# The second pair's last tile of a bilinear MLP as seven block products: its gate and up taken as the two rows of blocks, its weights summed anew, and the last output row written in halves

## The chip, the cores and the metric

The kernel runs on one core of a Trainium2 chip. The metric is the device time of one execution in microseconds. Three runs of the kernel before took 871.22, 871.30 and 872.47 us; the median is 871.3. A further execution was taken with the hardware profiler on and took 871.17 us; all rows below come from it. TensorE does the matmuls (PE; PEld is its weight load), VectorE (DVE), ScalarE (ACT) and GpSimd (POOL) do elementwise work, SyncE (SP) issues nearly all DMAs.

## The reference

All in float32, for one sequence of 2048 rows of 512. A layer norm with a shift and scale from a conditioning vector, a segmented attention with a memory (four segments of 512 rows), its residual, and then a second layer norm and a bilinear MLP with 1376 hidden columns:

```python
def _B_ref(x, w_gate, w_up, w_down):
    g = jnp.einsum("bsd,df->bsf", x, w_gate)
    u = jnp.einsum("bsd,df->bsf", x, w_up)
    h = g * u
    return jnp.einsum("bsf,fd->bsd", h, w_down)
...
    h = _layernorm(x, axis=-1) * (1 + ca) + sa
    x = x + ga * _A_ref(h, A_wq, A_wk, A_wv, A_wo, A_beta)
    h = _layernorm(x, axis=-1) * (1 + cb) + sb
    x = x + gb * _B_ref(h, B_w_gate, B_w_up, B_w_down)
```

Only the MLP is touched by the change.

## The kernel before, in words

**Precision.** A float32 product is made of three fast ones: each operand is split into a high part (`wh`, `bh`, a ScalarE copy that rounds) and a low part (`wl`, `bl`, a VectorE subtraction), and high by high, low by high and high by low are added up. Two halves of the contraction make it six matmuls (`six`, line 1259), always into one PSUM bank of 512 columns.

**Tiles.** The 2048 rows are four segments of 512, taken as two pairs, p = 0 and 1, with c = 0 and 1 for the segment in the pair. The 1376 hidden columns are tiles of 128, numbers 0 to 10; tile 10 (`LAST`) has 96. Tiles go in twos: a *unit* (`unit`, line 1386) makes one matrix, gate or up, of two tiles i and i+1 for both segments of the pair, that is a 2x2 block product (two tiles by two halves of the contraction, times two halves by two segments). It takes seven block products in place of eight (Winograd's form of Strassen's): pieces 1 to 7 of the rows (`pieces[p, j]`, made by `build`, line 1213) against seven sums of weight blocks (made by `wprep`, line 446, in the slots `wh`, `wl` of seven blocks; `WI` tells which product takes which). Products go in the order 2, 5, 1, 3, 6, and the last two, 7 and 4 (`seven`, `four`), are left in `tail` and run inside the next unit. Product 2 goes to bank Z, 5 and 3 to bank Y, 1, 6, 7 and 4 one upon the other to bank X; between them ScalarE copies Y and X out (`p5`, `p1`, `y`) and VectorE adds. TensorE may go on writing a bank only when these have read it.

**Order.** The units are, for pair 0, g2, u2, g4, ... u8 (n = 0 to 7), then n = 8 = `CH`, unit x: tile 10 of pair 1, gate and up; then pair 1's g2, u2, g4, u4, g6, u6, g8, u8, g0, u0 (n = 9 to 18). Tiles 0, 1 and 10 of pair 0 are done ahead of them all in the plain form with eight products (`open0`, `close0`, `other`, lines 1437 to 1463), and so is unit x (`x_unit`, line 1474): gate and up each take pieces 1, 2, 5, 3 against the plain halves of the weights, 8 products, 48 matmuls.

**Down.** When up is done, gate times up is split in high and low (`split`, `mids`), and eight down products (c, t) of the two tiles are queued in `dq`; each adds six matmuls in a bank `acc` (three for tile 10 alone) and VectorE adds that to the residual row `xa`. `d()` takes one from `dq` between the steps of a unit; `DS` (line 1570) lists at which steps. What is left runs at the end. Pair 0's rows are stored after their last addition and the tiles reloaded with pair 1's rows (`store`, `reload`).

**Weights.** Pair 0 keeps the prepared weights (of the units, of tile 10 and of w_down) in HBM (`keep`), pair 1 fetches them (`fetch`, line 400), and ScalarE must then copy each piece of a fetched tile once in place. `prepare(n)` (line 1484) is started two units ahead: it issues the DMAs of unit n, and for an up or x unit of w_down's tiles. A slot of unit weights is free when the unit three before has run its `four`. Tiles 0 and 1 of pair 1 are not kept; their sums are made anew.

**Queues.** Each engine takes its instructions in order. TensorE's order is written out (each matmul is tied to the one before it); `pin` ties an instruction of another engine behind the TensorE instruction issued last before it, and a planner in the build sets the order of ScalarE, VectorE and SP within these ties. An instruction that waits holds up all behind it on its engine.

Of the kernel before, what the change touches and what calls it, by code (L numbers as in the profile page):

```python
# [8 lines left out]
F32 = mybir.dt.float32  # L9
# [8 lines left out]
P = 128  # L18
# [39 lines left out]
def tile_kernel(ctx, tc, x, wq, wk_, wv, wo, beta, w_gate, w_up, w_down, c, w_mod, out):  # L58
# [20 lines left out]
    def pin(i):  # L79

        if last_pe[0] is not None:
            tc.add_manual_dep(i.ins, last_pe[0].ins.name, NOSYNC, reason="order")
# [328 lines left out]
    def xprep(n, tag, pool, rpool):  # L411

        wh = pool.tile([P, 7, 2, P], F32R, tag=f"wh{tag}", name=f"cwH{n}", bufs=1)
        wl = pool.tile([P, 7, 2, P], F32R, tag=f"wl{tag}", name=f"cwL{n}", bufs=1)
        m = ft[LAST][1]
        for j, nm in enumerate("gu"):
            plain[int(n == CH), LAST, nm] = wh[:, 0:4, j], wl[:, 0:4, j]
        flat = [a.rearrange("p a b c -> p (a b c)")[:, 0:8 * P] for a in (wh, wl)]
        if n == CH:
            yield from fetch(("x", LAST), flat, wkeep)  # L420
            return
        raw = rpool.tile([P, KT, 2, P], F32, tag="raw0", name=f"cr{n}", bufs=1)
        nc.gpsimd.memset(raw[:, :, :, m:], 0.0)
        for j, w in enumerate((w_gate, w_up)):
            pin(nc.sync.dma_start(raw[:, :, j, 0:m], w.rearrange("(k p) f -> p k f", p=P)[:, :, LAST * P:]))
        yield
        act.activation(wh[:, 0:4], raw, AF.Copy)
        vec.tensor_sub(wl[:, 0:4], raw, wh[:, 0:4].bitcast(F32))
        yield
        keep(("x", LAST), flat, wkeep)  # L430
        yield

    def prep(i, pool, rpool):
# [17 lines left out]
    def wprep(n, tag, pool, rpool):  # L451

        _, nm, i = units[n]
        if (nm, i) not in wkeep:
            raw = rpool.tile([P, KT, 2, P], F32, tag=f"raw{(n + 1) % 2}", name=f"cr{n}", bufs=1)
        wh = pool.tile([P, 7, 2, P], F32R, tag=f"wh{tag}", name=f"cwH{n}", bufs=1)
        wl = pool.tile([P, 7, 2, P], F32R, tag=f"wl{tag}", name=f"cwL{n}", bufs=1)
        wslot[n] = wh, wl
        if (nm, i) in wkeep:
            yield from fetch((nm, i), [a.rearrange("p a b c -> p (a b c)") for a in (wh, wl)], wkeep)  # L460
            return
        views = [w.rearrange("(k p) f -> p k f", p=P)[:, :, i * P:] for w in (w_gate, w_up)]
        pin(nc.sync.dma_start(raw.rearrange("p k r c -> p k (r c)"), views["gu".index(nm)][:, :, 0:2 * P]))
        yield
        S = rpool.tile([P, 4, 2, P], F32, tag="ws0", name=f"cs{n}", bufs=1)

        def A(r, c):
            return raw[:, 2 * c:2 * c + 2, r]

        def hi(d, v):  # L470
            pin(act.activation(wh[:, d], v, AF.Copy))

        def lo(d, v):
            pin(vec.tensor_sub(wl[:, d], v, wh[:, d].bitcast(F32)))

        top = slice(4, 6), raw[:, :, 0].rearrange("p (c k) f -> p c k f", c=2)
        low = 6, A(1, 1)
        s1, s2 = ((d, S[:, d]) for d in (slice(0, 2), slice(2, 4)))
        pin(vec.tensor_add(S[:, 0], A(1, 0), A(1, 1)))
        pin(vec.tensor_sub(S[:, 1], S[:, 0], A(0, 0)))  # L480
        hi(*top)
        yield
        pin(vec.tensor_sub(S[:, 2], A(0, 0), A(1, 0)))
        pin(vec.tensor_sub(S[:, 3], A(0, 1), S[:, 1]))
        hi(*low)
        hi(*s1)
        yield
        lo(*top)
        hi(*s2)
        yield  # L490
        lo(*low)
        lo(*s1)
        yield
        lo(*s2)
        yield
# [717 lines left out]
    def build(p):  # L1213

        def emit(j, srcs):
            pool = bc if j < 3 else pc
            hi = pool.tile([P, 2, L], F32R, tag=f"bh{j}", name=f"bH{p}_{j}", bufs=1)
            lo = pool.tile([P, 2, L], F32R, tag=f"bl{j}", name=f"bL{p}_{j}", bufs=1)
            for k in range(2):
                pin(act.activation(hi[:, k], srcs[k], AF.Copy))  # L1220
                pin(vec.tensor_sub(lo[:, k], srcs[k], hi[:, k].bitcast(F32)))
            pieces[p, j] = hi, lo

        T = pc.tile([P, 2, L], F32, tag="ws1", name=f"t{p}", bufs=1)

        def comb(a, b):
            for k in range(2):
                pin(vec.tensor_sub(T[:, k], a[k], b[k]))

        t = [T[:, k] for k in range(2)]  # L1230
        b11, b12, b21, b22 = ([hfs[2 * p + c, r][:, k] for k in range(2)] for r in range(2) for c in range(2))
        if p > 0:
            emit(2, b21)
            yield
        comb(b12, b11)
        yield
        if p > 0:
            emit(1, b11)
            yield
        emit(5, t)  # L1240
        yield
        emit(3, b22)
        yield
        comb(b22, t)
        yield
        emit(6, t)
        yield
        comb(b21, t)
        yield
        emit(4, t)  # L1250
        yield
        comb(b22, b12)
        yield
        emit(7, t)
        yield
# [64 lines left out]
    def down(p, fs, c, t):  # L1320
        while p == 1 and outs and fs[0] != ENDS[1]:
            store(0)
        while p == 1 and again:
            reload()
        ps = dbank(f"acc{p}_{fs[0]}_{c}_{t}")
        n = 3 * len(fs)
        j = 0
        for f in fs:
            m = ft[f][1]
            mH, mL = mids[p, f, c]  # L1330
            dH, dL = wds[p, f]
            for a, b in ((mH, dH), (mL, dH), (mH, dL)):
                pe(nc.tensor.matmul(ps, a[0:m, t * P:(t + 1) * P], b[0:m], start=j == 0, stop=j == n - 1))  # L1333
                j += 1
        xa = x1a[p, c, t]
        vec.tensor_add(xa, xa, ps)  # L1336
        if fs[0] == ENDS[p]:
            outs.append((c, t, xa))
            if p == 1:
                store(p)  # L1340
            else:
                if len(outs) > 1:
                    store(p)
                if len(again) > 2:
                    reload()
# [40 lines left out]
    def unit(n):  # L1386

        p, nm, i = units[n]
        wh, wl = wslot[n]
        u = f"{nm}{p}_{i}"  # L1390

        def mm(ps, j, first, last):
            six(ps, wh, wl, lambda k: (WI[j], k), P, *pieces[p, j], first, last)

        def out_of(name, ps):
            r = tmp(name)
            act.activation(r, ps, AF.Copy)
            return r

        Z = pst((P, 512), "sm", f"Z{u}")  # L1400
        mm(Z, 2, True, True)
# [5 lines left out]
        prev(0)  # L1407
        X = xbank(f"X{u}")
        mm(X, 1, True, True)
        finish(p, nm, i, 0, add(Z, out_of(f"p1{u}", X)), False)  # L1410
        yield 3
        mm(Y, 3, False, True)
        yy = out_of(f"y{u}", Y)
# [2 lines left out]
        tail.clear()  # L1416
        yield 5
        mm(X, 6, False, True)
        finish(p, nm, i, 1, add(X, yy), False)
        yield 6  # L1420

        def seven():
            mm(X, 7, False, True)
            finish(p, nm, i + 1, 1, add(X, p5), False)

        def four():
            mm(X, 4, False, True)
            finish(p, nm, i + 1, 0, X, True)
            if nm == "u":
                dq.extend(lambda c=c, t=t: down(p, (i, i + 1), c, t) for c in (1, 0) for t in range(4))  # L1430

        tail.extend((seven, four))

# [37 lines left out]
        ndir[0] += 1  # L1471
        return pst((P, 512), DB[(ndir[0] - 1) % 4], name)

    def x_unit(n):

        for st in open0(1, LAST):
            yield st
            prev(0)
            tail[0:1] = []
        yield from close0(1, LAST)  # L1480
        yield from other(1, LAST)
        dq.extend(lambda c=c, t=t: down(1, (LAST,), c, t) for c in (0, 1) for t in range(4))

    def prepare(n):

        if n >= NU:
# [1 line left out]
        p, nm, i = units[n]  # L1488
        slot = -n % 3
        if (nm, i) in wkeep:  # L1490
            gens = [(xprep if nm == "x" else wprep)(n, slot, pc, pc)]
            gens += [wdprep(p, f) for f in {"g": (), "u": (i, i + 1), "x": (LAST,)}[nm]]
            for g in gens:
                next(g)
            yield
            for g in gens:
                yield from g
            return
        if nm == "x":
            yield from xprep(n, slot, pc, pc)  # L1500
            yield from wdprep(p, LAST)
            return
        yield from wprep(n, slot, pc, pc)
        if nm == "u":
# [62 lines left out]
        next(nb)  # L1567
    run(pr0)
    dq.extend(lambda f=f, t=t: down(0, f, 1, t) for f in ((LAST,), (0, 1)) for t in range(4))
    DS = {"g": (1, 2), "u": (1, 2, 3, 4, 5, 6), "x": (1, 2, 4)}  # L1570
    lgs = []

    def lns():
# [5 lines left out]
    for n in range(NU):  # L1579
# [4 lines left out]
            keep((nm, i), [a.rearrange("p a b c -> p (a b c)") for a in wslot[n]], wkeep)  # L1584
        if n == CH - 1:
            nb = build(1)
        for st in (unit if nm != "x" else x_unit)(n):
            next(old, None)
            if wait:
                if st == 4:  # L1590
# [6 lines left out]
                next(nb, None)  # L1597
            if n == 0:
                d(1 + st % 2 if st > 1 else 1)
            elif st in DS[nm] and n < NU - 1:  # L1600
                d()
            if 3 <= n < CH - 1:
                next(lg, None)
                if st > 4:
# [45 lines left out]
```

## Time and profile before

| | us |
|---|---|
| median of three runs | 871.3 |
| profiled execution | 871.17 |
| its span, first to last instruction | 869.5 |
| TensorE busy | 841.8 (97%) |
| VectorE busy | 645.1 (74%) |
| ScalarE busy | 496.7 (57%) |
| start of unit x on TensorE | 679.05 |
| start of g2 of pair 1 on TensorE | 701.39 |
| end of the last matmul | 865.60 |
| last row's addition, its store's issue | 865.63, 866.35 |

Times in rows are microseconds from the span's start. A row of the chain gives start, duration, engine, bank, line and number of matmuls; a row of a timeline the engine, line, operation, out<-in, and in brackets the idle time before it with what ended it; a row of DMA issues the KB each and the microseconds from issue to landing. Names are as in the kernel, without numbers: Xg is bank X of a gate unit, `cwL<-keptLu` the fetch of the low parts of an up unit's weights. Matmul records can be missing here and there, and matmuls overlap, so their spacing is read from starts.

### The profile page before, as it was taken

Reading aid. Unit: us, or ns where it says so; the run is one execution under the profiler, and the core shown is the slowest. Engines: PE = TensorE matmul, PEld = TensorE weight load, DVE = VectorE, ACT = ScalarE, POOL = GpSimd, SP = SyncE. Lnnn points to the kernel's source line nnn. Section 1 sums busy time; section 2 is a strip of 40 time slices with the busy share of each in tenths; the row PEclk is TensorE's granted clock in tenths of the full one; section 3 lists DMA queues with packets and bytes.
Section 4 is the critical chain, followed back from the end, with each engine's and each line's share of the span. In section 5 each row is a group of like instructions: output and inputs, shape, how many; then the busy total and the mean of one; then the engine's idle time right before and its main releaser. Section 6 shows DMA issues by size and latency. Waiting matters only on the chain.

```text
span 869.5 us, 14406 instructions
## 1 busy us (share of the span) xinstructions
PE 841.8 (97%) x4975; PEld 598.1 (69%) x4976; DVE 645.1 (74%) x1792; ACT 496.7 (57%) x755; POOL 275.5 (32%) x424
## 2 busy tenths in 40 slices
PE   8989999999999999999999999999999999999998
PEld 5755656565665565665666677788888778888886
DVE  7698766887778877778879457989987936447654
ACT  3757757677777686677545626344536645554430
POOL 4545535466546574586424610000000000000000
PEclk9999999999999999999999999999999999999999
DMA  7555443546436454557476349569552665443012
GB/s 235 159 165 131 127 110 98 177 127 177 124 98 177 129 134 129 134 148 233 131 231 192 123 156 309 206 209 340 197 210 98 221 237 198 167 140 139 36 49 97
DMA packets 83304, 141.28 MB, mean 162 GB/s; under 512 B 11712, under 2 KB 45504, under 8 KB 83232
## 3 DMA queue, kind: packets, MB, share of 16 engines
q1 hardware_dynamic: 83088, 140.35, 51.4%
q8 instruction: 39, 0.64, 0.3%
q14 instruction: 33, 0.27, 0.1%
q10 hardware_dynamic: 144, 0.02, 0.0%
HBM read 90.52 MB, written 49.55 MB: 161 GB/s over the span
## 4 chain that ended last, share of the span: by engine, by line
PE 80%; DVE 12%; ACT 5%; issue 1%; DMA 1%; ACTq 0%
PE acc L1333 14%; PE tb L85 8%; PE Xu L1264 7%; PE Xg L1264 7%; PE k L85 6%; PE q L85 6%; DVE q L39 6%; PE vps L85 5%; PE wops L85 5%; PE Yu L1264 4%; PE Yg L1264 4%; PE qps L85 3%; PE kps L85 3%; ACT pt L324 2%; PE Zg L1264 1%; PE Zu L1264 1%
## 5 line engine op out<-in xcount | busy, mean ns | idle before, releaser
L39 DVE CUSTOM_DVE_ANT_0 q<-q,cmask 128x384 f32<-128x384 f32 (+3 forms) x512 | 245.7, 508 | 60.8 <-PE q L85 52.9
L324 ACT ACTIVATE pt<-k 128x1024 f32<-128x1024 f32 x160 | 163.8, 1024 | 65.1 <-PE k L85 64.7
L330 POOL TENSOR_SCALAR_AFFINE_SELECT pt<-pt 128x256 f32<-128x256 f32 (+1 forms) x224 | 97.5, 449 | 167.2 <-ACT pt L324 166.9
L85 PE MATMUL q<-kst,qst 96*128 96x384 bf16 (+3 forms) x512 | 103.3, 298 | 12.5 <-DVE nm L39 11.2
L85 PE MATMUL k<-qst,kst 98*128 98x384 bf16 (+3 forms) x512 | 97.1, 302 | 4.4 <-ACT pt L324 4.2
L1336 DVE TENSOR_TENSOR xa<-xa,acc 128x512 f32<-128x512 f32 x96 | 65.4, 683 | 46.9 <-PE acc L1333 46.5
L85 PE MATMUL tb<-pt,v 128*32 128x512 f32 (+3 forms) x1024 | 75.5, 436 | 0.0
L39 DVE DVE_READ_ACCUMULATOR2_ANT nm<- 128x1 f32 x512 | 71.8, 140 | 0.0
L85 PEld LDWEIGHTS <-kst 98*128 98x128 bf16 x512 | 37.7, 98 | 48.7 <-issue 42.8
L85 PEld LDWEIGHTS <-qst 96*128 96x128 bf16 x512 | 45.6, 97 | 34.8 <-issue 12.4
L1333 PE MATMUL acc<-dH,mH 128*128 128x512 f32 (+1 forms) x152 | 60.3, 397 | 0.0
L1333 PE MATMUL acc<-dL,mH 128*128 128x512 f32 (+1 forms) x152 | 60.1, 395 | 0.0
L1333 PE MATMUL acc<-dH,mL 128*128 128x512 f32 (+1 forms) x152 | 60.0, 395 | 0.0
L85 PEld LDWEIGHTS tb<-pt,v 128*32 128x32 f32 x1024 | 28.7, 109 | 38.6 <-issue 35.1
L356 ACT ACTIVATE tsb<-tb 128x512 f32<-128x512 f32 x32 | 19.0, 595 | 40.2 <-PE tb L85 40.1
L1333 PEld LDWEIGHTS acc<-dL,mH 128*128 128x128 f32 (+1 forms) x152 | 28.6, 188 | 7.1
L1333 PEld LDWEIGHTS acc<-dH,mL 128*128 128x128 f32 (+1 forms) x152 | 28.5, 188 | 7.1 <-DVE mL L1284 0.3
L1333 PEld LDWEIGHTS acc<-dH,mH 128*128 128x128 f32 (+1 forms) x152 | 28.5, 188 | 6.7
L85 PE MATMUL kps<-ahH,wkH 128*128 128x512 f32 x64 | 30.2, 473 | 0.0
L85 PE MATMUL wops<-woH,oH 128*128 128x512 f32 x64 | 28.2, 441 | 0.7 <-ACT oH L519 0.7
L85 PE MATMUL qps<-ahH,wqH 128*128 128x512 f32 x64 | 28.7, 449 | 0.0
L85 PE MATMUL vps<-wvH,ahH 128*128 128x512 f32 x64 | 28.3, 442 | 0.0
(376 smaller groups left out, 2024.7 us busy)
## 6 DMA issues: line engine op xcount, KB each, us to landing
wm<-in_w_mod_dram SPq DMA_DIRECT2D x24, 256.0 KB, 4.2
kd<-k SPq DMA_DIRECT2D x16, 384.0 KB, 2.6
kst<-kd SPq DMA_DIRECT2D x32, 192.0 KB, 3.2
qd<-q SPq DMA_DIRECT2D x16, 384.0 KB, 2.8
qst<-qd SPq DMA_DIRECT2D x32, 192.0 KB, 3.7
x<-in_x_dram SPq DMA_DIRECT2D x16, 256.0 KB, 4.3
kst<-kd SPq DMA_DIRECT2D x32, 128.0 KB, 3.2
qst<-qd SPq DMA_DIRECT2D x32, 128.0 KB, 3.7
```

The lines of the kernel that those rows point to most:

```text
L39: i = getattr(self.eng, name)(*a, **k)
L85: return pe(nc.tensor.matmul(*a, **k))
L324: ex = act.activation(pt, kp, AF.Exp, scale=0.25)
L330: sels[u, i] = nc.gpsimd.affine_select(w, w, pattern=[[0, w.shape[1]], [1, P]], compare_op=ALU.is_ge, fill=0.0, base=0, channel_multiplier=-1)
L356: act.activation(tsbs[u], tbs.pop(u), AF.Copy)
L1264: pe(nc.tensor.matmul(ps[0:n], a, b[:, k], start=first and c == 0, stop=last and c == 5, skip_group_check=True))
L1333: pe(nc.tensor.matmul(ps, a[0:m, t * P:(t + 1) * P], b[0:m], start=j == 0, stop=j == n - 1))
L1336: vec.tensor_add(xa, xa, ps)
```

## The change

Unit x goes through `unit` like the others. Its two rows of blocks are not two tiles of one matrix but the gate and the up of tile 10: block row 0 is gate, row 1 is up. `cell(r, c, ...)` hands the four results to `finish` as gate for r = 0 and up for r = 1, so that one unit gives both. All its operands have 96 columns or rows (`m`).

Its weights are no longer kept by pair 0 and fetched: `wprep` loads gate's and up's 96 columns once more (two DMAs of 192 KB), makes the four sums on VectorE and the high and low parts of the seven blocks. Pair 0's two stores of 512 KB go. `x_unit` goes.

As products 7 and 4 of u8 and of x now run in `tail` a unit later, `build` for pair 1 cuts its pieces 4 and 7 two steps later. `DS` is set anew: units x, g2 and u2 get lists of their own, gate units two down products at steps 1 and 2 as before, up units one at each of the six steps. Tile 10's down products of pair 1 go in the order c = 1, then 0, like the others.

The last down product of the kernel, (c, t) = (0, 3) of tiles 0 and 1, adds and stores its row in two halves of 256 columns, the first store issued from ScalarE's queue and the second from SP's.

```diff
@@ xprep (now for pair 0 alone)
-            plain[int(n == CH), LAST, nm] = wh[:, 0:4, j], wl[:, 0:4, j]
-        flat = [a.rearrange("p a b c -> p (a b c)")[:, 0:8 * P] for a in (wh, wl)]
-        if n == CH:
-            yield from fetch(("x", LAST), flat, wkeep)
-            return
+            plain[0, LAST, nm] = wh[:, 0:4, j], wl[:, 0:4, j]
...
-        yield
-        keep(("x", LAST), flat, wkeep)
@@ wprep
+        m = ft[i][1]
...
-        pin(nc.sync.dma_start(raw.rearrange("p k r c -> p k (r c)"), views["gu".index(nm)][:, :, 0:2 * P]))
+        if nm == "x":
+            for j in range(2):
+                pin(nc.sync.dma_start(raw[:, :, j, 0:m], views[j]))
+        else:
+            pin(nc.sync.dma_start(raw.rearrange("p k r c -> p k (r c)"), views["gu".index(nm)][:, :, 0:2 * P]))
@@ build
+        if p > 0:
+            yield
+            yield
         emit(4, t)
-        yield
+        if p == 0:
+            yield
         comb(b22, b12)
@@ down
         xa = x1a[p, c, t]
+        if p == 1 and fs[0] == ENDS[1] and (c, t) == (0, 3):
+            for q, h in ((nc.scalar, slice(0, D // 2)), (nc.sync, slice(D // 2, D))):
+                vec.tensor_add(xa[:, h], xa[:, h], ps[:, h])
+                q.dma_start(out[rows(2 * p + c, t), h], xa[:, h])
+            return
         vec.tensor_add(xa, xa, ps)
@@ unit
+        def cell(r, c, v, psum):
+            if nm == "x":
+                finish(p, "gu"[r], i, c, v, psum)
+            else:
+                finish(p, nm, i + r, c, v, psum)
...
-            if nm == "u":
-                dq.extend(lambda c=c, t=t: down(p, (i, i + 1), c, t) for c in (1, 0) for t in range(4))
+            if nm != "g":
+                fs = (i,) if nm == "x" else (i, i + 1)
+                dq.extend(lambda c=c, t=t: down(p, fs, c, t) for c in (1, 0) for t in range(4))
@@ x_unit: removed
@@ the loop over the units
-    DS = {"g": (1, 2), "u": (1, 2, 3, 4, 5, 6), "x": (1, 2, 4)}
+    DS = {"g": (1, 1, 0, 0, 0, 0), "u": (1,) * 6, CH: (1, 1, 0, 0, 1, 2), CH + 1: (1, 1, 1, 1, 1, 1), CH + 2: (2, 1, 1, 1, 1, 1)}
-        for st in (unit if nm != "x" else x_unit)(n):
+        for st in unit(n):
-            elif st in DS[nm] and n < NU - 1:
-                d()
+            elif n < NU - 1:
+                d(DS[n][st - 1] if n in DS else DS[nm][st - 1])
```

More of the change, by code (lines that the diff above doesn't have):

```diff
@@ L461, in wprep @@
             return
+        m = ft[i][1]
         views = [w.rearrange("(k p) f -> p k f", p=P)[:, :, i * P:] for w in (w_gate, w_up)]
-        pin(nc.sync.dma_start(raw.rearrange("p k r c -> p k (r c)"), views["gu".index(nm)][:, :, 0:2 * P]))
+        if nm == "x":
[3 more added lines that the diff above has]
+            pin(nc.sync.dma_start(raw.rearrange("p k r c -> p k (r c)"), views["gu".index(nm)][:, :, 0:2 * P]))
         yield
-        S = rpool.tile([P, 4, 2, P], F32, tag="ws0", name=f"cs{n}", bufs=1)
+        S = rpool.tile([P, 4, 2, P], F32, tag="ws0", name=f"cs{n}", bufs=1)[:, :, :, 0:m]
+        wh, wl, raw = wh[:, :, :, 0:m], wl[:, :, :, 0:m], raw[:, :, :, 0:m]
         def A(r, c):
@@ L1390, in unit @@
         u = f"{nm}{p}_{i}"
+        m = ft[i][1]
         def mm(ps, j, first, last):
-            six(ps, wh, wl, lambda k: (WI[j], k), P, *pieces[p, j], first, last)
+            six(ps, wh, wl, lambda k: (WI[j], k), m, *pieces[p, j], first, last)
         def out_of(name, ps):
             r = tmp(name)
-            act.activation(r, ps, AF.Copy)
+            act.activation(r[0:m], ps[0:m], AF.Copy)
             return r
+        def cell(r, c, v, psum):
[3 more added lines that the diff above has]
+                finish(p, nm, i + r, c, v, psum)
         Z = pst((P, 512), "sm", f"Z{u}")
@@ L1409, in unit @@
         mm(X, 1, True, True)
-        finish(p, nm, i, 0, add(Z, out_of(f"p1{u}", X)), False)
+        cell(0, 0, add(Z, out_of(f"p1{u}", X), m), False)
         yield 3
@@ L1418, in unit @@
         mm(X, 6, False, True)
-        finish(p, nm, i, 1, add(X, yy), False)
+        cell(0, 1, add(X, yy, m), False)
         yield 6
@@ L1423, in seven @@
             mm(X, 7, False, True)
-            finish(p, nm, i + 1, 1, add(X, p5), False)
+            cell(1, 1, add(X, p5, m), False)
         def four():
             mm(X, 4, False, True)
-            finish(p, nm, i + 1, 0, X, True)
-            if nm == "u":
-                dq.extend(lambda c=c, t=t: down(p, (i, i + 1), c, t) for c in (1, 0) for t in range(4))
+            cell(1, 0, X, True)
+            if nm != "g":
+                fs = (i,) if nm == "x" else (i, i + 1)
+                dq.extend(lambda c=c, t=t: down(p, fs, c, t) for c in (1, 0) for t in range(4))
         tail.extend((seven, four))
@@ L1472, in dirbank @@
         return pst((P, 512), DB[(ndir[0] - 1) % 4], name)
[L1474 to L1482, printed above, removed]
     def prepare(n):
@@ L1490, in prepare @@
         if (nm, i) in wkeep:
-            gens = [(xprep if nm == "x" else wprep)(n, slot, pc, pc)]
-            gens += [wdprep(p, f) for f in {"g": (), "u": (i, i + 1), "x": (LAST,)}[nm]]
+            gens = [wprep(n, slot, pc, pc)]
+            gens += [wdprep(p, f) for f in {"g": (), "u": (i, i + 1)}[nm]]
             for g in gens:
@@ L1499, in prepare @@
         if nm == "x":
-            yield from xprep(n, slot, pc, pc)
-            yield from wdprep(p, LAST)
+            gens = [wprep(n, slot, pc, pc), wdprep(p, LAST)]
+            for g in gens:
+                next(g)
+            yield
+            for g in gens:
+                yield from g
             return
```

## The prediction, made before the changed kernel was run

> **What bounds the kernel.** I read the page's busy shares first, then the busy time by stretch, then the chain that ended last, and then the queues of ScalarE and of the DMA issues around the tile that is changed.
>
> ```profile
> PE 841.8 (97%) x4975; PEld 598.1 (69%) x4976; DVE 645.1 (74%) x1792; ACT 496.7 (57%) x755; POOL 275.5 (32%) x424
> ```
>
> The stretches (columns: PE, PEld, DVE, ACT, POOL busy, then clock, DMA share, GB/s):
>
> ```profile
> 560.00:679.05 119.05, 119.05 (x533) 96.62 (x531) 104.08 (x198) 55.54 (x101) 0.00 (x0) 1.00 0.59 214
> 679.05:865.60 186.55, 186.54 (x805) 149.50 (x803) 106.60 (x167) 82.86 (x129) 0.00 (x0) 1.00 0.40 141
> ```
>
> From the second pair's first matmul (679.05) to the last of the kernel (865.60) TensorE has no gap: 805 matmuls in 186.55 us, 0.232 us from start to start, at a granted clock of 1.00. So here a matmul less is 0.23 us less, and any wait of TensorE is paid in full. The chain names the pieces, six matmuls a piece:
>
> ```profile
> 679.21 1.37 PE Xg L1264 x6
> ...
> 834.90 1.36 PE Xg L1264 x6
> ...
> 843.19 22.42 PE acc L1333 x96
> ```
>
> A product of six lasts 1.36 to 1.40 us, with 96 columns of weights (the first row) or 128.
>
> **The change, part by part.** *The products.* The eight products of tile 10 become seven: 48 matmuls to 42. Six times 0.232 is 1.39. Worked by kind it is hardly other: four products on pieces 1 and 2 become two, four on pieces 5 and 3 become two, and 6, 7 and 4 are new; the cheapest product (1.36) and the dearest (1.40) bound it. I take -1.4.
>
> *The weights.* Gone: two stores and two fetches of 512 KB and two conversions on ScalarE. New: two loads of 192 KB, four sums and four low parts on VectorE, four high parts on ScalarE, and one more addition in the unit itself.
>
> ```profile
> L474 DVE TENSOR_TENSOR cwL<-cs,cwH 128x512 fp32r<-128x512 f32 x20 | 13.2, 682 | 0.0
> L479 DVE TENSOR_TENSOR cs<-cr 128x256 f32<-128x256 f32 x10 | 4.2, 416 | 1.7 <-DMA cr<-in_w_gate_dram 1.6
> ```
>
> ```profile
> 660.00:680.00 20.00, 16.57 (x28) 1.00 0.37 129
> ```
>
> The new operations are 192 or 384 wide, so on VectorE at most five of 0.42 and three of 0.68: 4.1 us, some of it before 660 and about 1.9 us of low parts after it, where VectorE (its busy time alone, in the second fence) has 3.4 us free in 20. The high and low parts can't begin before u6's last product has read the slot, which the old fetch waited for too. I place the low parts at 660 to 663, which pushes the first addition behind them by 2 to 3 us; TensorE asks for nothing of them before 679. Price 0; without that cover it would be the 1.9. ScalarE changes two conversions for four shorter ones: 0.
>
> *The pieces.* Pieces 4 and 7 of pair 1 are cut later, behind u8's last product, but are first used a unit later than now (about 701 and 708); by VectorE's queue they are there near 698. Price 0, up to 0.5 if VectorE is late.
>
> *The down products.* Eighteen stand in the units x, g2, u2 where fourteen did, so the stock is used up at u2: g4 has none, and the end has 16 (of them 2 between the last products of u0) instead of 18. Their number is the same. The residual rows are now stored and reloaded in the order in which they are added; the shortest way from a row's last use in pair 0 to its first in pair 1 grows from 42 matmuls to 75, that is from 10 to 17 us. Price 0.
>
> *The wait that this makes, in g4.* TensorE runs ahead of ScalarE there. ScalarE takes work in order, and the conversions of fetched weights stand ahead of the copy that frees TensorE's bank. The rows now:
>
> ```profile
> 722.29 1.38 PE Xg L1264 x6
> ...
> 736.15 1.36 PE Xg L1264 x6
> ```
>
> ```profile
> 723.63 1.12 SPq L402 DMA_DIRECT2D cwL<-keptLu  x1
> 724.85 0.38 SPq L402 DMA_DIRECT2D cwH<-keptHu  x1
> ```
>
> ```profile
> 729.87 1.06 ACT L408 ACTIVATE cwL<-cwL 128x1024 fp32r<-128x1024 f32 x1 [1.43 <-DMA cwL<-keptLu]
> 730.84 0.58 ACT L1397 ACTIVATE p5g<-Yg 128x512 f32<-128x512 f32 x1
> 732.07 1.79 ACT L408 ACTIVATE cwH<-cwH 128x1024 fp32r<-128x1024 f32 x2 [0.65 <-DMA cwH<-keptHu]
> 733.77 0.83 ACT L408 ACTIVATE cwL<-cwL 128x768 fp32r<-128x768 f32 x1
> 734.50 0.62 ACT L408 ACTIVATE dH<-dH 128x512 fp32r<-128x512 f32 x1
> 735.02 0.58 ACT L1397 ACTIVATE p1g<-Xg 128x512 f32<-128x512 f32 x1
> ```
>
> Time from T, the start of g2's last product (722.29). The fetch for u4 is issued when it ends (T+1.34); Xg's sixth product, at T+13.86, must not write before the copy p1g has read the bank (T+13.3). So 0.5 us is spare. The change takes two half down products (2 x 0.70) out of that stretch: Xg now stands at T+12.47. What ScalarE does first stays the same, with mH of yg (0.53) moved behind the first conversion. With the low part of the weights landing 5.8 us after its issue, as in the next fetch of u-weights (749 to 760, fence below), ScalarE starts at T+7.1; then 0.97, 0.53, 0.48, 0.73, 1.70 and 0.52, from start to start in the rows above, bring p1g to T+12.1 and its end, 0.6 later, to T+12.7.
>
> ```profile
> cwL<-keptLu SPq DMA_DIRECT2D x1, 896.0 KB, 5.8
> cwH<-keptHu SPq DMA_DIRECT2D x1, 896.0 KB, 7.6
> ```
>
> TensorE waits 0.2 to 0.3. With the 6.2 us that 723.63 to 729.87 shows it would be 0.65; with a landing under 5.5 us, nothing. I take 0.3 (now a reload of a residual row is issued just ahead of this fetch; changed, it isn't), bounds 0 and 0.7.
>
> *The same in g0.* The fetch of w_down's tiles 0 and 1 waits for the last down product of tiles 6 and 7 to have read its weights; that product moves from the end (840.40) into g0 (to the place of 819.67), and three conversions then stand ahead of g0's copy p1g, which Xg's sixth product needs.
>
> ```profile
> 819.67 1.40 PE acc L1333 x6
> ...
> 826.60 1.36 PE Xg L1264 x6
> ...
> 840.40 1.40 PE acc L1333 x6
> ```
>
> ```profile
> 846.41 0.63 ACT L408 ACTIVATE dH<-dH 128x512 fp32r<-128x512 f32 x1
> ```
>
> Xg's sixth stands 6.93 us after that down product starts. The same four fetches let ScalarE begin the third conversion at +6.0 (846.41 - 840.40); p1g follows at +6.5 and ends at +7.1: a wait of 0.2. The same four fetches behind the last down product of tiles 4 and 5 (801.53) let the third conversion begin sooner, at +4.9, and leave none:
>
> ```profile
> 806.38 0.63 ACT L408 ACTIVATE dH<-dH 128x512 fp32r<-128x512 f32 x1 [0.23 <-DMA dH<-keptHd]
> ```
>
>  In g6 and g8 only one conversion stands ahead of p1g: 2 us to spare. I take 0.15, bounds 0 and 0.4.
>
> *The last row.* Two additions of 256 columns in place of one, and two stores of 128 KB, the first from ScalarE's queue.
>
> ```profile
> 865.63 0.69 DVE L1336 TENSOR_TENSOR xa<-xa,acc 128x512 f32<-128x512 f32 x1 [0.71 <-PE acc L1333]
> 866.35 0.33 SPq L1351 DMA_DIRECT2D out_dram<-xa  x1
> ```
>
> ```profile
> out_dram<-xa SPq DMA_DIRECT2D x1, 256.0 KB, 2.0
> qst<-nt SPq DMA_DIRECT2D x64, 4.0 KB, 1.7
> ```
>
> Two of 0.42, 0.35 apart, end 0.08 later than one of 0.69. A store of 256 KB lands after 2.0 us, one of 4 KB after 1.7, so one of 128 KB saves about 0.15. I take -0.1, bounds -0.4 (all of the 0.3 saved, a shorter end) and +0.3 (a second queue to be waited for, which no row shows). The Trainium skill ("DMA: Bandwidth & Descriptors", latency and other measured facts) puts most of a DMA's roughly 2 us down to the round trip to memory, whatever the size; by that halving would save nothing and this step would be +0.1, the sum 0.2 higher.
>
> **The sum.** -1.4 + 0.3 + 0.15 - 0.1 = -1.05 us. The profiled execution took 871.17 (span 869.5 and 1.67 around it), 0.13 under the median of 871.3. So 870.1, and against the median 870.2: 0.13% less. The measurement tells about 0.2%, 1.7 us, from no change.
>
> **The rivals.** *No new wait:* the fetch lands early enough in g4 and g0. -1.4 - 0.1 = 869.7, and with the tail's best bound 869.4. For it: both waits are a few tenths, and the g4 one ends with a landing under 5.5 us. Against: the landing of these weights is 5.8 and 6.2 in the rows above.
>
> *ScalarE gives it all back:* the g4 wait at its bound (0.7), g0 at 0.4, and 0.3 in the tail: 871.1. For it: 6.2 us is what this very fetch took. Against: its disturber is gone.
>
> *Slower:* in unit x ScalarE now has the two conversions of w_down's tile 10 ahead of the copy p1x, and behind that the high part that the first down product of pair 8 needs at 691.0. The fetch is issued near 684.1: 0.9 us after the start of the down product whose weights it overwrites, as at 685.65 against 684.74, and that product now starts near 683.2, eighteen matmuls after 679.05.
>
> ```profile
> 684.74 1.40 PE acc L1333 x6
> ```
>
> ```profile
> 685.65 0.38 SPq L402 DMA_DIRECT2D dL<-keptLd  x1
> ```
>
> ```profile
> dL<-keptLd SPq DMA_DIRECT2D x1, 256.0 KB, 2.8
> ```
>
> With 2.8 us to land it is converted at 687.6, p1x is copied by 688.2, added by 688.9, the low part cut by 689.6: 1.4 spare. Every microsecond beyond a landing of 4.2 is paid in full; slower by 0.2% needs 7 us or more, as two 256 KB stores in its way would have to make it: 873.1 then. Against: the 2.8 of the same fetch.
>
> *A matmul less is worth less than its spacing:* if weight loads set the pace, the six would be worth only their own loads.
>
> ```profile
> L1264 PEld LDWEIGHTS Xu<-bL,cwH 128*128 128x128 f32 (+1 forms) x42 | 7.8, 187 | 1.9
> ```
>
> Six of 0.187 are 1.1: 870.5. The spacing of 0.232 over 805 matmuls speaks against it. The Trainium skill ("TensorE: Matmul & The Clock Gate", back-to-back issue gap) gives 131 ns a matmul of 512 columns in a stream with weight loads; by it the six would be worth 0.8. The trace has 0.232.
>
> **How the numbers follow.** The sum as it stands: 0.48. No new wait: 0.23. All given back: 0.16. Slower in unit x: 0.07. Worth less: 0.02. What I don't see: 0.04. Faster by over 0.2% (under 869.56) are half of the second case, a little of the first at its bounds and half of the unseen: 0.17. Slower by over 0.2% (over 873.0): 0.09. Within: 0.74. The range takes the first three and the small one: 869.4 (no wait, best tail) to 871.6 (all given back, half a microsecond of the wait in unit x).
>
> **What would show it.** Right: 42 products' matmuls of tile 10, no gap of TensorE between 640 and 720, a gap of some 0.3 us ahead of the sixth product of g4 and one of 0.2 or less in g0, the rest at 0.232 from start to start, and the last matmul about 1 us earlier. Wrong: a gap in unit x or g2 put down to ScalarE or VectorE, a spacing other than 0.232, or a longer way from the last matmul to the end than now (3.9 us).

## The result

The changed kernel takes 870.96 us in the median of 12 runs (869.22 to 872.34); the kernel before, run beside it, 872.12 (871.22 to 873.52). The ratio is 0.9983 with a 95% interval of 0.9975 to 0.9991: 1.5 us less, between 0.8 and 2.2 (the two medians themselves lie 1.2 apart). That is inside 0.2%, by a little, and the interval reaches beyond it. The kernel before ran 0.8 slower beside it than the 871.3 that the forecast of 870.2 started from, so the differences are to be compared, not the times: 1.05 less was forecast.

The page's busy shares of the changed kernel:

```profile
PE 840.5 (97%) x4969; PEld 598.1 (69%) x4970; DVE 649.4 (75%) x1802; ACT 495.9 (57%) x757; POOL 276.3 (32%) x424
```

TensorE has six matmuls less. The stretch from the first matmul of the second pair to the last of the kernel (same columns as before) shows it without a gap again, 799 matmuls where 805 stood:

```profile
678.69:863.75 185.06, 185.03 (x799) 148.36 (x797) 107.47 (x168) 81.86 (x129) 0.00 (x0) 1.00 0.40 141
```

The chain that ended last, changed kernel (start, length, engine, what, matmuls):

```profile
675.91 1.39 PE Xu L1268 x6
...
723.21 1.38 PE Xg L1268 x6
...
735.65 1.36 PE Xg L1268 x6
...
827.53 1.36 PE Xg L1268 x6
...
844.12 19.62 PE acc L1337 x84
863.74 0.02 issue
863.76 0.42 DVE xa L1342
```

676 us is the best point to measure from: there the last product that the first pair's unit u8 runs itself (Xu) starts, ahead of unit x, and all that follows is one unbroken row of matmuls in both kernels. I call the time from there to the end of the last matmul the *way*. It is 863.74 - 675.91 = 187.83; the same product started at 676.43 in the kernel before, whose last matmul ended at 865.61:

```profile
676.43 1.39 PE Xu L1264 x6
```

189.18, so 1.35 us went between these two points. From the last matmul to the end of the span it is 3.76 us where it was 3.87. Those two make 1.46, and the ratio says 1.5. The spans of the two profiles differ by 2.0 (867.5 against 869.5), but 0.5 of this lies before the first matmul of the MLP, in unchanged code: over the thirteen profiles of this study that matmul starts between 517.85 and 520.26.

In g4, where a wait of 0.3 us was forecast, the list of TensorE's waits has no line after 519 us, and the sixth product stands 735.65 - 723.21 = 12.44 us behind T (the start of g2's last product), just where the matmuls put it. ScalarE was in time, because the low weights came sooner. The issue on SP's queue, the DMA's time to landing, and ScalarE's work (in g4, then in g0):

```profile
724.43 0.32 SPq L402 DMA_DIRECT2D cwL<-keptLu  x1
```

```profile
cwL<-keptLu SPq DMA_DIRECT2D x1, 896.0 KB, 4.4
```

```profile
728.89 1.06 ACT L408 ACTIVATE cwL<-cwL 128x1024 fp32r<-128x1024 f32 x1 [3.61 <-DMA cwL<-keptLu]
...
733.79 0.58 ACT L1407 ACTIVATE p1g<-Xg 128x512 f32<-128x512 f32 x1
...
826.04 0.63 ACT L408 ACTIVATE dH<-dH 128x512 fp32r<-128x512 f32 x1 [0.86 <-DMA dH<-keptHd]
826.58 0.58 ACT L1407 ACTIVATE p1g<-Xg 128x512 f32<-128x512 f32 x1
```

The copy p1g of g4 ends at 734.37, 1.28 before the product that needs its bank; that of g0 at 827.16, 0.37 before. These count as the forecast did, from the chain's rows, which put a product's start at the modelled end of the matmul before it. The product's own first matmul starts 0.16 sooner, so that by it 1.12 and 0.21 are spare:

```profile
735.49 0.39 PE L1268 MATMUL Xg<-bH,cwH 128*128 128x512 f32 x1
```

So the course was that of the rival "no new wait". Two questions are left for the chip: whether the 1.35 is the product and nothing else, and why the weights landed after 4.4 us and not 5.8.

### The profile page after: what moved, and what is told of

The parts are those of the page before. It is cut to its first block, busy times and chain, and to the rows that moved or that the text cites. A ratio compares the mean times of both kernels' runs of the same rounds, so it can differ in the third digit from the quotient of the medians.

```text
span 867.5 us, 14401 instructions
## 1 busy us (share of the span) xinstructions
PE 840.5 (97%) x4969; PEld 598.1 (69%) x4970; DVE 649.4 (75%) x1802; ACT 495.9 (57%) x757; POOL 276.3 (32%) x424
## 4 chain that ended last, share of the span: by engine, by line
PE 81%; DVE 12%; ACT 5%; issue 1%; DMA 0%; DVEq 0%; ACTq 0%
PE acc L1337 14%; PE tb L85 8%; PE Xu L1268 7%; PE Xg L1268 7%; PE k L85 6%; PE q L85 6%; DVE q L39 6%; PE vps L85 5%; PE wops L85 5%; PE Yu L1268 4%; PE Yg L1268 4%; PE qps L85 3%; PE kps L85 3%; ACT pt L324 2%; PE Zg L1268 1%; PE Zu L1268 1%
```

## The experiments

All beside the kernel before on the same chip. Way and tail (last matmul's end to the end of the span) are from the profiles, the tail from the times as the traces keep them, since the page rounds a span to 0.1:

| kernel | median us | ratio to before (95%) | way | tail |
|---|---|---|---|---|
| before | 872.1 to 872.8 | 1 | 189.18 | 3.87 |
| changed | 870.96 | 0.9983 (0.9975 to 0.9991) | 187.83 | 3.76 |
| changed, again | 870.44 | 0.9981 (0.9972 to 0.9990) | 187.82 | 3.75 |
| product twice | 871.38 | 0.9994 (0.9985 to 1.0003) | 189.18 | 3.76 |
| last row whole | 870.87 | 0.9981 (0.9972 to 0.9991) | 187.82 | 3.77 |
| before, row in halves | 871.94 | 0.9996 (0.9987 to 1.0005) | 189.18 | 3.63 |
| stores kept | 870.48 | 0.9973 (0.9964 to 0.9983) | 187.86 | 3.64 |
| memory tiles kept | 869.45 (one run) | | 187.85 | 3.63 |
| copies x3, x2 | 872.65 (one run) | | 190.41 | 3.76 |
| copies x6, x4 | 879.70 | 1.0080 (1.0065 to 1.0095) | 196.02 | 3.75 |
| two products less | 867.47 | 0.9939 (0.9920 to 0.9957) | 187.82 | 3.76 |
| one product more | 871.64 (one run) | | 187.82 | 3.76 |
| down products even | 871.93 | 0.9991 (0.9979 to 1.0002) | 189.34 | 3.75 |

(The two kernels with products less and more differ in the first pair, ahead of the way.)

**The changed kernel again.**

> The changed kernel itself once more, so that the others of this group have it on the same chip. It should stand 1.2 to 1.8 us under the kernel before (about 0.17%); the way from the second pair's first matmul to the last one should again take 185.05 us against 186.40. If the 1.35 us between these two was an accident of one profile, this row comes out differently by a few tenths.

The way is 187.82 against 187.83: one profile tells it to a few hundredths of a microsecond, where the medians tell half a microsecond at best.

**The product.** In the unit of tile 10:

```diff
         Z = pst((P, 512), "sm", f"Z{u}")
         mm(Z, 2, True, True)
+        if nm == "x":
+            mm(Z, 2, True, True)
```

> The changed kernel with the second of the seven products of tile 10 done twice into the same bank (the second time starts the sum anew, so the output is the same): 48 matmuls there again, with everything else of the change kept. Theory one, the gain between the first and the last matmul of the second pair is the product alone: 1.36 to 1.40 us back, the way is 186.4 us, and the time stands 0 to 0.2 us under the kernel before (all that is left is the tail). Theory two, the gain comes from the order of the down products, the dropped stores or the dropped fetches, and a product less is hidden anyway: the way stays at 185.1 to 185.5 and the time stays within 0.4 us of the changed kernel's.

```profile
676.26 1.39 PE Xu L1268 x6
...
679.04 2.73 PE Zx L1268 x12
```

The twelve matmuls stand in the chain, and the way is 189.18, that of the kernel before to the hundredth. So the whole gain of the way is the six matmuls, 1.35 us or 0.225 each; the other order of the down products, the weights summed anew and the dropped stores are worth nothing there. This also ends the rival that a matmul is worth only its weight load (0.187, 1.1 in all). By the Trainium skill ("TensorE: Matmul & The Clock Gate", back-to-back issue gap) it would have been 0.8; the trace disagrees.

**The last row.** Whole again in the changed kernel, and, the other way round, halves in the kernel before:

```diff
-        if p == 1 and fs[0] == ENDS[1] and (c, t) == (0, 3):
-            for q, h in ((nc.scalar, slice(0, D // 2)), (nc.sync, slice(D // 2, D))):
-                vec.tensor_add(xa[:, h], xa[:, h], ps[:, h])
-                q.dma_start(out[rows(2 * p + c, t), h], xa[:, h])
-            return
         vec.tensor_add(xa, xa, ps)
```

> The changed kernel with the last row added and stored whole again. Theory one, the halves save what the profile shows: from the last matmul's end to the end of the span 3.9 us in place of 3.76, the time 0.1 to 0.15 us above the changed kernel's. Theory two, a store takes the same whatever its size, and the halves save nothing: 3.7 to 3.8 us, or the time 0.1 us below the changed kernel's. The median of the times can hardly tell 0.1 us; the rows of the tail can.

> The kernel before with its last row summed and stored in halves, nothing else. Theory one: the tail is 3.76 us in place of 3.89, the time 0.1 to 0.15 us under the kernel before, and the way from the second pair's first matmul to the last one stays 186.40. Theory two: the halves bring more than the trace of one execution showed, up to 0.4 us (of the 1.48 us between the medians, 1.35 are the product), which would show as 0.3 us or more under the kernel before.

The medians can't tell this, as expected, and the tails hardly can: 3.87 and 3.77 us whole, 3.63 to 3.76 in halves (eleven profiles, mean 3.72), and in the changed kernel 3.77 whole against 3.76 and 3.75 in halves. What follows the last store's landing takes 1.01 to 1.15 us in these profiles, whole or in halves, and covers the difference. The landing itself tells it. The last store's issue, first whole (last matmul's end at 865.70), then in halves in the changed kernel (863.74):

```profile
866.44 0.33 SPq L1355 DMA_DIRECT2D out_dram<-xa  x1
```

```profile
864.54 0.33 SPq L1343 DMA_DIRECT2D out_dram<-xa  x1
```

The stores in the changed kernel landed after 1.8 us each, where the one of 256 KB took 2.0:

```profile
out_dram<-xa ACTq DMA_DIRECT2D x1, 128.0 KB, 1.8
out_dram<-xa SPq DMA_DIRECT2D x1, 128.0 KB, 1.8
```

So the last landing is 2.60 to 2.61 us behind the last matmul's end in all eleven profiles in halves and 2.76 in both with the row whole: 0.15 less. How much of it reaches the end of the span isn't settled by two profiles of the whole row; the means say 0.1. With the prediction's reading of the Trainium skill ("DMA: Bandwidth & Descriptors", latency and other measured facts), that halving a store saves nothing, the landing would have come about 0.1 later, and no profile shows that. The reading took the fixed cost for the whole: beside it the Trainium skill (same title, Anatomy of one DMA) has a part that grows with the bytes.

**Why the weights landed early: stores or addresses.** The change drops two stores of 512 KB, and with them two tiles in memory, so that all later kept tiles lie elsewhere. First both back, then the tiles with an eighth of the store:

```diff
         yield
+        keep(("x", LAST), [a.rearrange("p a b c -> p (a b c)")[:, 0:8 * P] for a in (wh, wl)], {})
+        yield
```

```diff
         yield
+        for x, a in zip("HL", [a.rearrange("p a b c -> p (a b c)")[:, 0:8 * P] for a in (wh, wl)]):
+            k = dram.tile([P, 8 * P], F32, name=f"kept{x}x{LAST}")
+            nc.sync.dma_start(k[:, 0:P], a[:, 0:P].bitcast(F32))
+        yield
```

> The changed kernel with the two stores of 512 KB of tile 10's weights in the first pair kept, as the kernel before has them (nobody reads them; the memory tiles for them stand where they stood, so the later tiles lie at the addresses of before). The question is why the low weights of u4 landed 4.4 us after their issue and not 5.8 to 6.2, which is what made the forecast wait of 0.3 us in g4 vanish. Theory one, the stores or the addresses set the landing: u4's low part lands at 5.7 to 6.2 again, the copy p1g of g4 ends within 0.3 us of the sixth product's place, and the time is 0 to 0.4 us above the changed kernel's. Theory two, it is the reload of a residual row that stood in front of the fetch and is now elsewhere: the landing stays at 4.4 to 4.7, the copy keeps its 1.28 us of spare, and the time is the changed kernel's.

> The changed kernel with the same two memory tiles set aside but only an eighth of each stored (64 KB). If the addresses set the landing of the kept weights, u2 to u8 land here as in the run with the whole stores, tile by tile; if the traffic of the stores does, they land as in the changed kernel (u2 4.5, u4 4.4, u6 5.6, u8 4.5 us for the low parts). The time should be that of the changed kernel in either case.

u4's low weights with the stores back:

```profile
cwL<-keptLu SPq DMA_DIRECT2D x1, 896.0 KB, 4.5
```

4.5 in the second kernel too, and u6 and u8 as in the changed kernel (5.6 and 4.4 to 4.5). Neither the stores nor the addresses set the landing; theory one is out.

**Is the spare true?** ScalarE's copy p1g repeated, three times in g4 and twice in g0, then six and four times:

```diff
-            act.activation(r[0:m], ps[0:m], AF.Copy)
+            for _ in range({"p1g1_4": 3, "p1g1_0": 2}.get(name, 1)):
+                act.activation(r[0:m], ps[0:m], AF.Copy)
```

> The changed kernel with ScalarE's copy p1g done three times over in g4 and twice in g0 (same result). It measures the spare that the trace shows: 1.28 us in g4, 0.37 in g0. One more copy is 0.52 us. Theory one, those spares are true: g4 uses 1.04 of its 1.28 and has no gap of TensorE; g0 goes 0.15 over and shows a gap of 0.1 to 0.2. Theory two, the bank is asked for sooner or later than the chain's rows say: a gap in g4 too, or none in g0.

> The changed kernel with the copy p1g done six times over in g4 and four times in g0 (same result). In g4 one conversion of w_down (0.47) also falls between the copies. Theory one, TensorE waits for this copy alone and every microsecond beyond the spare is paid in full: g4 is 5 x 0.52 + 0.47 - 1.28 = 1.8 late at most (1.2 without the conversion), g0 3 x 0.52 - 0.37 = 1.2; both are seen as gaps ahead of the sixth product, and the time is 2.3 to 3 us above the changed kernel's. Theory two, the wait is hidden by other work of TensorE or made up later: the time rises by less than 1 us.

Both expectations were too low, since the order written by the planner puts other work of ScalarE between the copies. TensorE's waits and the chain in g4 of the first:

```profile
PE Xg L1268 <- ACT p1g L1408: 2.0, 2, 1.2
```

```profile
734.64 0.48 ACT p1g L1408
735.13 0.09 ACT mH L1287
735.21 0.33 issue
735.54 0.59 ACT yg L1408
736.13 0.50 ACT p1g L1408
736.63 0.02 issue
736.65 0.61 ACT p1g L1408
737.26 0.04 issue
737.30 1.66 PE Xg L1268 x6
```

With that work counted, the spares fit. In g4 the first copy ended at 735.12 by ScalarE's rows, 1.39 before the sixth product's place (724.07 + 12.44 = 736.51), and the last one at 737.26: 2.14 later, so 0.75 too late; the wait is 0.78. In g0 the last copy came 1.53 after the first, with 0.36 to spare, and the wait is 1.2. So the bank is asked for where the chain says, and a copy that is late by more than its spare is paid in full; the forecast's mechanism holds. The longer version has waits of 6.1 in all and is slower by 0.8%:

```profile
PE Xg L1268 <- ACT p1g L1408: 6.1, 2, 3.2
```

A wait costs more than its row says. The way of the first grew by 2.58, with 2.0 of waits; that of the second by 8.19 (196.02 - 187.83), with 6.1. In the first each pause carries 0.3 on top. Of this 0.16 is how the row counts: from the modelled end of the matmul before, while in the full stream the next one starts 0.16 ahead of that end (matmuls of 0.39 start 0.23 apart). The other 0.11 are in the first matmul after the pause, which takes 0.50 and has the next one 0.34 behind it. In the second the pause of 3.2 us in g4 brought the clock down (the granted clock is the third column from the end; first row g4 just after its pause, second row g0 after its own):

```profile
741.25:744.25 3.00, 2.97 (x7) 2.39 (x8) 0.70 (x2) 1.53 (x3) 0.00 (x0) 0.50 0.90 364
...
837.85:840.60 2.75, 2.74 (x12) 2.25 (x13) 1.48 (x3) 0.00 (x0) 0.00 (x0) 1.00 0.00 0
```

Seven matmuls at half the clock, 3.15 us from start to start for what takes 1.6; the pause of 2.96 in g0 of the same run left the clock at 1.00. The trace has the half clock from 741.04 to 744.46, for 3.4 us. The Trainium skill ("TensorE: Matmul & The Clock Gate", Part 1) says that TensorE falls to half its clock after about 3.4 us without work, in a window that runs freely, and needs as long to come back; the half clock and its length fit. The fall came sooner, 2.94 us behind the modelled end of the last matmul (738.10), and the pause of 2.96 brought none, so here the length of a pause doesn't decide alone. That the place of the window decides with it would fit; two pauses don't show it.

**Why the weights landed early: the transfers of instructions.** The trace lists, beside the kernel's own DMA queue, transfers of kind instruction: on queue 8 one of 16 KB every 27 to 33 us in this part. In the changed kernel one starts at 752.32, 1.5 us behind the issue of u6's low weights (750.82), which land after 5.6 us; the share in the row of the quarter microsecond from 752.25 (26.5% of 16 engines) is 1.06 us on one engine:

```profile
q8 instruction: 1, 0.02, 26.5%
```

While u6's weights are fetched, the DMA share is 1.00 to 1.05 (753 to 756), so all 16 engines are full. That a fetch spread over them has landed only when the last one is done, and a transfer on one of them so holds it up, is an inference, and the next two kernels try it. To move these transfers against the work, two products of the first pair are left out in one kernel, and one is done twice in the other:

```diff
-        mm(Y, 3, False, True)
+        if u not in ("g0_8", "u0_8"):
+            mm(Y, 3, False, True)
```

```diff
         mm(Y, 5, True, True)
+        if u == "g0_8":
+            mm(Y, 5, True, True)
```

> The changed kernel with two products (of piece 3, in the gate and the up part of the first pair's tiles 8 and 9) left out, so its output is not the reference's. In the runs so far a fetch of 896 KB of u-weights landed 1.2 us later whenever one of the 16 KB transfers of kind instruction (one every 29 us of TensorE's work, about 1 us on one DMA engine) fell into its packets: 9 of 9 fetches fit. Two products less put those transfers 2.8 us later against the work. Theory one, they set the landing: the one near u4's fetch moves from 2 us ahead of the fetch's issue to 0.9 behind it, and the low weights land after 5.6 to 5.7 us in place of 4.4; the one near u8's moves likewise, 4.5 becomes 5.7. ScalarE's copy p1g of g4 then ends within 0.1 us of the sixth product's place: no wait, or one of 0.1. Theory two, something else that the change moved sets it (the reload of a residual row, the down products): u4 and u8 stay at 4.4 and 4.5. The time falls by the products, 2.7 to 2.8 us under the changed kernel's, in both.

> The changed kernel with one product of the first pair's tile 8 (piece 5, gate) done twice into the same bank (the output is the same). It puts the transfers of kind instruction 1.4 us earlier against the work. Theory one: the one that falls into u6's fetch now (1.4 us behind its issue) comes at or before its first packet, and u6's low weights land after 4.4 in place of 5.6, u4's and u8's stay at 4.2 to 4.5. Theory two: u6 stays at 5.6. The time is 1.4 us above the changed kernel's.

With one product more the transfer starts at 751.27, 2.0 us ahead of u6's issue (753.26), and u6's weights land after 4.4:

```profile
q8 instruction: 1, 0.02, 27.3%
...
cwL<-keptLu SPq DMA_DIRECT2D x1, 896.0 KB, 4.4
```

With two less, the one near u8 starts at 781.90, 1.1 behind the issue (780.80), and u8's land after 5.5 in place of the changed kernel's 4.5:

```profile
q8 instruction: 1, 0.02, 33.4%
...
cwL<-keptLu SPq DMA_DIRECT2D x1, 896.0 KB, 5.5
```

u4 was a miss of the first expectation: its transfer moved by only 1.6 us, to 0.3 ahead of the issue, and the landing stayed at 4.4, so the case that was to be made didn't come about (and with it no wait in g4). u6's moved to 5.0 behind the issue, when the low part had landed (4.5), and now the high part was late (7.5, else 6.2). The time of the kernel with two less, 5.3 us under the kernel before by the ratio (3.8 to 7.0), has room for the products' 2.8 beside the change's 1.5.

Taken together, for the low weights of u4, u6 and u8 in all kernels of the table but the last: twelve fetches with such a transfer starting 1.1 to 2.9 us behind their issue landed after 5.53 to 5.85 us, twenty-two where it started earlier or later after 4.22 to 4.54. Left out of this is u4 in the kernel before, with its reload (6.2, and 6.0 with the row in halves). There the transfer started 0.3 and 0.2 us ahead of the issue, about where it stood for u4 with two products less, which landed after 4.4; so it isn't what made these two late. Shown is that these transfers, moved with nothing else of this part changed, move the landing by 1.0 to 1.2 us.

**The places of the down products.** The change gives the units of tile 10 and u2 uneven numbers of down products. Made even:

```diff
-    DS = {"g": (1, 1, 0, 0, 0, 0), "u": (1,) * 6, CH: (1, 1, 0, 0, 1, 2), CH + 1: (1, 1, 1, 1, 1, 1), CH + 2: (2, 1, 1, 1, 1, 1)}
+    DS = {"g": (1, 1, 0, 0, 0, 0), "u": (1,) * 6, CH: (1,) * 6}
```

> The changed kernel with the down products spread over unit x, g2 and u2 one after each product, as in the other units, in place of the counts that the change gives (x: 1, 1, 0, 0, 1, 2; u2: 2, 1, 1, 1, 1, 1), so that fewer stand in u2. The number of all products is the same. Theory one, TensorE is full and their places are worth nothing as long as nothing comes late: the way from the second pair's start to the last matmul stays 185.05 within 0.1, no wait of TensorE. Theory two, the counts are needed to cover the new unit's sums and cuts: a wait of TensorE for VectorE or ScalarE shows in unit x or g2, and the time rises by that.

Neither theory. Units x and g2 have no wait, but g4 has one:

```profile
PE Yg L1268 <- ACT p5g L1407: 1.1, 1, 1.1
```

```profile
cwH<-keptHu SPq DMA_DIRECT2D x1, 896.0 KB, 8.4
cwL<-keptLu SPq DMA_DIRECT2D x1, 896.0 KB, 10.2
```

```profile
722.25 8.44 DMA cwH<-keptHu
...
732.51 0.49 ACT p5g L1407
733.00 0.04 issue
733.04 1.66 PE Yg L1268 x6
```

u4's fetch now stands right behind four fetches of w_down and a reload on SP's queue, high part first; it lands after 8.4 us, its conversion stands ahead of the copy p5g on ScalarE, and TensorE waits for the bank. The way is 189.34, 1.5 longer: all that the product gains. A 16 KB transfer fell into this fetch too (2.1 us behind the low part's issue), but it is not all: in this kernel the low weights of u6 and u8 landed after 6.6 and 6.7 us with no 16 KB transfer in their packets, behind 256 KB fetches issued 1.0 and 0.8 us ahead, which the changed kernel doesn't have there. Which of the transfers ahead does what was not taken apart.

## Why the prediction was right, and where it wasn't

*Products, -1.4.* Right: 1.35, shown to be the six matmuls alone.

*The wait in g4, +0.3.* This step failed. The mechanism is as told (the repeated copies show that the bank is paid for in full once the spare is gone), but the landing that was put in, 5.8 us, came from u6's fetch, which had a transfer of instructions in its packets. Without one such a fetch lands after 4.4, and that is what u4's now does: 1.28 us spare and no wait. The rest of the working held: from the start of the first conversion to that of p1g it is 4.90 us (728.89 to 733.79), forecast 4.93. With such a transfer, 1.2 of the spare would be gone and the wait still 0.1 at most (worked out; no kernel made this case). The 6.2 of the kernel before is a third case: a 256 KB reload issued 0.4 us ahead, and an issue that itself took 1.12; that these two make it was argued, not tried. The 6.6 and 6.7 behind fetches of 256 KB, in the kernel with even down products, point the same way.

*The wait in g0, +0.15.* Mis-sized by the same kind of step: the third conversion begins 5.44 us after the down product (826.04 - 820.60), not 6.0, and 0.37 us are spare. The two rows it was judged by gave 6.0 and 4.9, and I took the later.

*Weights and pieces, 0.* Right: no wait in unit x or g2, and the way is that of the products. VectorE cut the low parts from 659.82 to 662.17, where the forecast put them, and the last piece was ready at 696.51, forecast near 698.

*Down products, 0.* Right for the change, but the reason was too light. Their places aren't free: spread evenly they bring a wait of 1.1 us in g4, at another bank than the forecast named.

*Last row, -0.1.* Right: -0.11 between the two profiles and 0.1 between the means, with the landing 0.15 sooner. The reason holds too: a store of 128 KB lands 0.2 sooner than one of 256 KB, and the two additions end 0.06 later than one.

*The sum.* -1.05 forecast, about -1.5 measured; "no new wait", -1.5, was the course, with 0.23 of the chance. A difference within 0.2% was called likeliest and came, near its edge. Of the signs named for the forecast, the six matmuls, the stretch without a gap and the spacing came, and the gaps in g4 and g0 didn't. So the time lies in the range by a rival's course, and that the weights met no transfer of instructions in g4 was luck, worth 0.1 us at most by the working above.

*Slower in unit x.* No trace of it: the fetch of w_down's tile 10 was issued at 683.75 and the copy p1x began at 687.22. Both are 0.4 sooner than forecast because the unit starts 0.36 sooner in this profile; from the unit's start they are on it.

## What to carry to other kernels

Where TensorE has no gap, count its matmuls and look for a fixed point late in the chain to measure from: the way from there told 0.04 us (seven kernels with the same work gave 187.82 to 187.86) where the medians told 0.5. When the time of a fetch decides between a wait and none, don't take one row of its kind: look at what else moved in its packets, transfers of instructions included, and price the step for both cases. A forecast of zero for moved work holds only as long as the fetches that it lets go keep their places in the queue.

## What was not expected of the hardware

A 16 KB transfer of kind instruction, about 1 us on one DMA engine, makes a 896 KB fetch that it falls into land about 1.2 us later (5.53 to 5.85 us in place of 4.22 to 4.54); it comes every 27 to 33 us and moves when TensorE's matmuls ahead of it are more or fewer, so it looks like TensorE's own instructions, which is an inference. A pause of TensorE of about 1 us costs 0.3 us more than its row in the profile, 0.16 of it by the way the row counts, and one of 3.2 us brought the half clock for 3.4 us, while one of 2.96 did not.
